# One load in eight: w1 of a decode kernel fetched as eight transfers of sixteen rows

## The chip, the cores and the metric

The kernel runs on 1 core of a Trainium2 chip. The metric is device time in microseconds (us), from one execution of the whole program; lower is better. Three runs of the kernel before took 1298.88 us each.

## What is computed

One decode step of an attention block, gated by a small MLP, for B = 2 tokens of width D = 512. H = 32 heads of 128 attend to a cache of 8192 keys and values each; everything is float32. Cut to what matters, the reference is:

```python
xn = layernorm(x)
q  = (xn @ wq).reshape(B, 1, 32, 128).transpose(0, 2, 1, 3)
p  = softmax(einsum("bhqd,bhkd->bhqk", q, k_cache) / sqrt(128))
s  = einsum("bhqk,bhkd->bhqd", p, v_cache).transpose(0, 2, 1, 3).reshape(B, 1, 4096) @ wo
y  = layernorm(xn)
h  = gelu(y @ w1 + b1)          # w1: 512 x 1376
g  = silu(h @ w2 + b2)          # w2: 1376 x 512
out = x + s * g
```

The two caches are 268 MB each, the four weights together some 22 MB. Each byte of them is used once.

## The kernel before

A list of operations is written out by hand in program order; a small planner (`Plan`) finds for each of them, from the names that it reads and writes, which semaphores of other engines or of DMAs it has to wait for, and emits each engine's operations in that order. All loads are issued by SP (`load`, line 329) into one hardware DMA queue, which the 16 DMA engines of the core work off; each load has a semaphore by the name that it is given.

The start (up to some 60 us). SP issues, without a wait, w1, x, w2, b1, b2, wq, and the two halves of the first k tile:

```python
def load(dst, src, sem, w, over=()):
    op("sp", lambda: nc.sync.dma_start(dst, src), (), w, over=over, dma=sem)
load(w1_sb, w1.rearrange("(p c) f -> p c f", p=P), "w1", ["w1"])
load(x_sb, x.rearrange("b s d -> (b s) d"), "x", ["x"])
load(w2_sb, w2.rearrange("f n -> (f n)").rearrange("(p e) -> p e", p=P), "w2", ["w2"])
```

w1 stands in SBUF as 128 partitions of 4 x 1376 numbers: partition p holds rows 4p to 4p+3 of w1, 22,016 consecutive bytes of the source. w2 has the same size (2752 KB). Both lie, with all small tiles of the MLP, inside `vb`, the buffer that later takes the v tiles; so the trace calls w1, w2, x and the biases all `vb`. w1 and w2 read there as `in_B_w_dram`, b1 and b2 as `in_B_b_dram`.

DVE and ACT make the two layer norms of x (L380 to L385), PE transposes them (L392) and ACT copies the transposes out (L393). `hidden` multiplies the second one, yT, by w1 in three column blocks of four matmuls each (L435), adds b1 (L437), turns the rows into columns (L443, L449), applies the gelu, and spreads x over partitions (L460, L478). Then PE multiplies by wq (L518), which lies in k's first buffer, repeats q over the partitions (L531, ACT's copies L533), and does the product with w2 (`outer`, L487).

The loop. The work is cut into 32 tiles, one for each token and pair of heads. A tile of k is 128 partitions of 128 keys of 128 numbers (8.4 MB); DVE multiplies it by q (L559, two halves) and sums (L566), PE, ACT and DVE make the softmax of the tile, and PE weighs the v tile (L610, 32 matmuls, each in two passes in the trace). k has two buffers, v one. SP loads v of tile n when PE has weighed v of tile n-1, and k of tile n+2 when DVE is done with tile n; `load_v` names all that lay in `vb` at the start (the list `boot`) as overwritten. The end is the load of wo in seven pieces, the matmuls with it (L690 to L711), one DVE operation (L725) and the store.

Of the kernel before, what the change touches and what calls it, by code (L numbers as in the profile page):

```python
# [21 lines left out]
class Plan:  # L22
# [18 lines left out]
    def op(self, eng, fn, r=(), w=(), over=(), it=None, loop=False, dma=None):  # L41


        o = Op()
        o.eng, o.fn, o.it, o.loop, o.dma, o.tell = eng, fn, it, loop, dma, False
        need = {}

        def after(d, war):
            if d.dma is None and dma is None and d.eng == eng and (eng == "pe" or war):
                return  # L50
            if d.dma is None:
                if need.get(d.eng) is None or need[d.eng].idx < d.idx:
                    need[d.eng] = d
            else:
                k = ("dma", d.dma)
                if need.get(k) is None or need[k].idx < d.idx:
                    need[k] = d

        for k in r:
            if k in self.writer:  # L60
                after(self.writer[k], False)
        for k in list(w) + list(over):
            if k in self.writer:
                after(self.writer[k], False)
            for d in self.readers.get(k, ()):
                after(d, True)
        clock = self.clock[eng]
        need = {k: d for k, d in need.items() if clock.get(k, 0) < d.idx}
        o.deps = [(k, d) for k, d in need.items()
                  if not any(e is not d and e.done.get(k, 0) >= d.idx for e in need.values())]  # L70
        for _, d in o.deps:
            for k, v in d.done.items():
                clock[k] = max(clock.get(k, 0), v)
        own = eng if dma is None else ("dma", dma)
        self.count[own] = o.idx = self.count.get(own, 0) + 1
        o.done = dict(clock)
        o.done[own] = o.idx
        for k in w:
            self.writer[k] = o
            self.readers[k] = []  # L80
        for k in r:
            if k not in w:
                self.readers.setdefault(k, []).append(o)
        self.ops.append(o)
# [80 lines left out]
def decode_kernel(nc, x, kc, vc, wq, wo, w1, b1, w2, b2, out):  # L165
    P = 128
    B, H, S, DH = kc.shape
    D = x.shape[2]
    F = w1.shape[1]
    ND = D // P  # L170
# [32 lines left out]
    def pe(fn, r=(), w=(), it=None, loop=False):  # L203
        op("pe", fn, r, w, it=it, loop=loop)

    def dve(fn, r=(), w=(), it=None, loop=False, over=()):
        op("dve", fn, r, w, over=over, it=it, loop=loop)

    def act(fn, r=(), w=(), it=None, loop=False):
        op("act", fn, r, w, it=it, loop=loop)  # L210
# [4 lines left out]
    def sbuf(name, shape):  # L215
        return nc.alloc_sbuf_tensor(name, shape, F32).ap()
# [8 lines left out]
    vb = sbuf("vb", [P, KP * DH])  # L225
    kbuf = [t.rearrange("p (j d) -> p j d", d=DH) for t in kb]
    vbuf = vb.rearrange("p (j d) -> p j d", d=DH)
# [45 lines left out]
    boot = []  # L273

    def take(name, p, n, base=0, at=None):

        if at is None:
            at = used[0]
            used[0] += n
            assert used[0] <= KP * DH  # L280
        boot.append(name)
        return vb[base:base + p, at:at + n]

    w1_sb = take("w1", P, ND * F).rearrange("p (c f) -> p c f", f=F)
    w2_sb = take("w2", P, WB * P)

    at = used[0]
# [16 lines left out]
    yT = take("yT", P, ND * B).rearrange("p (c b) -> p c b", b=B)  # L304
# [13 lines left out]
    def bank():  # L318
        i = turn[0] % 4
        turn[0] += 1  # L320
        return scratch[i], f"s{i}"
# [3 lines left out]
    vf = vc.rearrange("b h s d -> (b h s d)").rearrange("(n p j d) -> n p j d", p=P, j=KP, d=DH)  # L325
    M = KP // 2

    def load(dst, src, sem, w, over=()):
        op("sp", lambda: nc.sync.dma_start(dst, src), (), w, over=over, dma=sem)  # L329
# [12 lines left out]
    CUT = D - P  # L342


    load(w1_sb, w1.rearrange("(p c) f -> p c f", p=P), "w1", ["w1"])
    load(x_sb, x.rearrange("b s d -> (b s) d"), "x", ["x"])
    load(w2_sb, w2.rearrange("f n -> (f n)").rearrange("(p e) -> p e", p=P), "w2", ["w2"])
    for t, src, k in ((b1_sb, b1, "b1"), (b2_sb, b2, "b2")):
# [79 lines left out]
    def hidden():  # L428

        chunks = range(0, F, 512)  # L430
        for f in chunks:
            w = min(512, F - f)
            ph, k = bank()
            for c in range(ND):
                pe(lambda f=f, w=w, ph=ph, c=c: matmul(ph[:B, :w], yT[:, c, :], w1_sb[:, c, f:f + w],  # L435
                                                       start=(c == 0), stop=False), ["yT", "w1"], [k])
            pe(lambda f=f, w=w, ph=ph: matmul(ph[:B, :w], ones[R:R + 1, :B], b1_sb[:, f:f + w],  # L437
                                              start=False, stop=True), ["ones", "b1"], [k])
            act(lambda f=f, w=w, ph=ph: nc.scalar.copy(h_nat[:, 1 + f:1 + f + w], ph[:B, :w]),  # L439
                [k, "h_nat"], [("h_nat", f)])  # L440

        for m in range(QT):
            dve(lambda m=m: nc.vector.tensor_copy(  # L443
                h_row[:, :, m::QT],
                h_nat[:, WM * m:WM * m + WB * R].rearrange("b (k e) -> b e k", e=WB)[:, :WR, :]),
                ["h_nat"] + [("h_nat", f) for f in chunks], [("h_row", m)])
        ph, k = bank()
        for r in range(WR):
            pe(lambda r=r: transpose(ph[:, r * B:(r + 1) * B], h_row[:, r, :], ident[2 * R:2 * R + B, 2 * R:2 * R + B]),  # L449
               ["ident"] + [("h_row", m) for m in range(QT)], [k])  # L450

        act(lambda: nc.scalar.copy(h, ph[:, :WR * B].rearrange("p (r b) -> p r b", b=B)), [k], ["h"])
        dve(lambda: nc.vector.tensor_mul(u, h, h), ["h"], ["u"])
        dve(lambda: nc.vector.tensor_scalar(u, u, GELU_A, 1.0, op0=ALU.mult, op1=ALU.add), ["u"], ["u"])
        dve(lambda: nc.vector.tensor_mul(u, u, h), ["u", "h"], ["u"])
        act(lambda: nc.scalar.activation(u, u, AF.Tanh, scale=GELU_C), ["u"], ["u"])
        dve(lambda: nc.vector.scalar_tensor_tensor(u, u, 1.0, h, op0=ALU.add, op1=ALU.mult), ["u", "h"], ["u"])
        dve(lambda: nc.vector.tensor_scalar_mul(u, u, 0.5), ["u"], ["u"])
        px, kx = bank()
        pe(lambda: matmul(px, pick, x_sb, start=True, stop=True), ["pick", "x"], [kx])  # L460
        act(lambda: nc.scalar.copy(xa, px), [kx], ["xa"])

        for c in range(QT):
            for lo, hi, r, m in ((0, c + 1, 1, QT - 1 - c), (c + 1, QT, 0, 0)):
                if lo == hi:
                    continue
                parts.append(("hs", c, lo))

                def part(c=c, lo=lo, hi=hi, r=r, m=m):
                    shape = [P, WM, hi - lo, B]  # L470
                    return nc.vector.tensor_tensor(
                        out=hs[:, :, c, lo:hi, :], in0=u[:, r:r + WM, :].unsqueeze(2).to_broadcast(shape),
                        in1=cls[:, m:m + hi - lo].unsqueeze(1).unsqueeze(3).to_broadcast(shape), op=ALU.mult)
                dve(part, ["u"] + [("cls", m) for m in range(QT)], [parts[-1]])
        dve(lambda: nc.vector.tensor_tensor(
            out=xa.rearrange("p (q n) -> p q n", n=CW), in0=xa.rearrange("p (q n) -> p q n", n=CW),
            in1=slot.unsqueeze(2).to_broadcast([P, CH, CW]), op=ALU.mult), ["xa", "slot"], ["xa"])
        dve(lambda: nc.vector.tensor_reduce(out=x4, in_=xa.rearrange("p (q n) -> p n q", n=CW), axis=AX.X, op=ALU.add),  # L478
            ["xa"], ["x4"])
# [20 lines left out]
    def gates():  # L500
        dve(lambda: nc.vector.scalar_tensor_tensor(th, th, 1.0, z, op0=ALU.add, op1=ALU.mult), ["th", "z"], ["th"])
        for j in range(QT):
            dve(lambda j=j: nc.vector.tensor_scalar_mul(  # L503
                gate[R * j:R * (j + 1), :, 1], th[R * j:R * (j + 1), j * CW:(j + 1) * CW], 0.5), ["th"], [("gate", j)])

    hidden()


# [3 lines left out]
    for i in range(NQ):  # L512
        for c in range(ND):
            wv = wq_sb[:, c, :].rearrange("p (h s d) -> p h s d", s=U, d=DH)
            a = (NQ - 1 - i) * B
            for j in range(QT):
# [4 lines left out]
                    start=(i + c == 0), stop=(i == NQ - 1 and c == ND - 1)),  # L521
                   ["xnT"] + [("kb", 0, s) for s in range(2)], ["po"])
    act(lambda: nc.scalar.copy(q_nat, PO), ["po"], ["o4"])
    for k in range(N // NB):
# [3 lines left out]
        p, kp = bank()  # L528
        for s in range(U):
            a = R * (U * g + s) + B * i + b  # L530
            pe(lambda p=p, s=s, a=a: matmul(p[HP * s:HP * (s + 1), :], ident[:, a:a + 1].to_broadcast([P, HP]), q_nat,  # L531
                                            start=True, stop=True), ["ident", "o4"], [kp])
# [6 lines left out]
    load_k(1)  # L539

    def load_v(n):
        load(vbuf, vf[n], "v", ["vb"], over=boot)

    def cols(t, a, n):

# [138 lines left out]
    def piece(c, n=0):  # L684
        return ("wo", max(i for i, a in enumerate(WO_PIECES[:-1]) if a <= c) + int(c == OC - 1 and n >= CUT))


    for c in range(WIDE):
        j = c % QT
        pe(lambda c=c, j=j: matmul(wide[R * j:R * j + RM, :], on[:, :, c], wo_sb[:, c, :],  # L690
                                   start=(c < QT), stop=(c + QT >= WIDE)), ["on", piece(c)], ["wide"])
# [9 lines left out]
    for c in range(WIDE, OC - LAST):  # L701
        for j in range(QT):
            pe(lambda c=c, j=j: matmul(acc[R * j:R * j + RM, :], on[:, :, c], wo_sb[:, c, j * P:(j + 1) * P],  # L703
                                       start=False, stop=(c == OC - LAST - 1)), ["on", piece(c)], ["acc"])
# [54 lines left out]
```

## Time and profile before

| | |
|---|---|
| runs | 1298.88, 1298.88, 1298.88 us |
| profiled execution | 1298.97 us, of which the span from the first to the last instruction is 1297.70 us |
| bytes moved | 559.33 MB in the one load queue |
| busiest engines | DVE 1138.0 us, PE 411.7 us |
| granted TensorE clock, mean | 0.626 |

How to read it: a row of the timeline has start, length, engine, line, operation, tiles (out<-in) and, in brackets, the idle time ahead of it and what ended it. A row of the windows has the window and its length, then each engine's busy time and number of instructions (PE, its weight loads, DVE, ACT, POOL), the granted clock, the mean busy share of the 16 DMA engines, and GB/s. Packets count in the window in which they start, so that short windows can show a share over 1.

### The profile page before, as it was taken

Reading aid. Unit: us, or ns where it says so; the run is one execution under the profiler, and the core shown is the slowest. Engines: PE = TensorE matmul, PEld = TensorE weight load, DVE = VectorE, ACT = ScalarE, POOL = GpSimd, SP = SyncE. Lnnn points to the kernel's source line nnn. Section 1 sums busy time; section 2 is a strip of 40 time slices with the busy share of each in tenths; the row PEclk is TensorE's granted clock in tenths of the full one; section 3 lists DMA queues with packets and bytes.
Section 4 is the critical chain, followed back from the end, with each engine's and each line's share of the span. In section 5 each row is a group of like instructions: output and inputs, shape, how many; then the busy total and the mean of one; then the engine's idle time right before and its main releaser. Section 6 shows DMA issues by size and latency. Waiting matters only on the chain.

```text
span 1297.7 us, 6944 instructions
## 1 busy us (share of the span) xinstructions
PE 411.7 (32%) x2796; PEld 123.9 (10%) x2796; DVE 1138.0 (88%) x294; ACT 78.0 (6%) x250; POOL 1.4 (0%) x8
## 2 busy tenths in 40 slices
PE   5602333312333312333311333321333321333327
PEld 1100011000101000101100101000001100001103
DVE  3699999888889988889988889988888988888991
ACT  1200000000000000000000000000000000000000
POOL 0000000000000000000000000000000000000000
PEclk9856666556666556666555666655666655666659
DMA  9999999999999999999999999999999999999998
GB/s 400 449 425 440 428 428 442 426 442 426 434 438 424 446 424 440 430 426 444 426 438 430 428 442 426 442 426 432 440 424 446 424 440 430 424 446 426 427 430 373
DMA packets 11231, 559.42 MB, mean 431 GB/s; under 512 B 1364, under 2 KB 1620, under 8 KB 1880
## 3 DMA queue, kind: packets, MB, share of 16 engines
q1 hardware_dynamic: 11224, 559.33, 99.7%
q8 instruction: 4, 0.07, 0.0%
q14 instruction: 3, 0.02, 0.0%
HBM read 559.30 MB, written 0.03 MB: 431 GB/s over the span
## 4 chain that ended last, share of the span: by engine, by line
DMA 72%; PE 23%; DVE 3%; issue 1%; ACT 0%; SPq 0%; another core or an unknown queue 0%; DVEq 0%; ACTq 0%
DMA vb<-in_A_v_cache_dram 67%; PE po L610 22%; DMA kb<-in_A_wq_dram 3%; DMA vb<-in_A_wo_dram 2%; DVE kb L559 1%; DVE sc L566 1%; PE po L518 1%; SPq L329 0%; PE acc L703 0%; PE s L531 0%; PE wide L711 0%; ACT PZ L587 0%; DVE gate L503 0%; PE s L582 0%; ACT Q L533 0%
## 5 line engine op out<-in xcount | busy, mean ns | idle before, releaser
L559 DVE TENSOR_TENSOR kb<-kb,Q 128x8192 f32<-128x8192 f32 x64 | 555.6, 8682 | 107.9 <-DMA kb<-in_A_k_cache_dram 96.7
L566 DVE TENSOR_REDUCE sc<-kb 128x64 f32<-128x8192 f32 x64 | 552.3, 8666 | 0.0
L610 PE MATMUL po<-vb,PZ 128*8 128x512 f32 x1984 | 288.8, 748 | 293.7 <-DMA vb<-in_A_v_cache_dram 292.0
L582 PE MATMUL s<-nm,srow 1*128 1x2 f32 x64 | 18.4, 355 | 364.1 <-DVE nm L576 364.1
L610 PEld LDWEIGHTS po<-vb,PZ 128*8 128x8 f32 x1984 | 57.5, 104 | 499.0 <-issue 497.2
L573 PE MATMUL s<-ident,mx 128*1 128x128 f32 x32 | 11.8, 369 | 180.2 <-DVE mx L570 180.2
L582 PEld LDWEIGHTS s<-nm,srow 1*128 1x128 f32 x64 | 15.7, 302 | 373.3 <-DVE nm L576 373.3
L617 ACT COPY o<-po 128x512 f32<-128x512 f32 x32 | 18.8, 586 | 541.7 <-PE po L610 541.7
L583 ACT COPY bias<-s 128x2 f32<-128x2 f32 x32 | 5.1, 160 | 609.3 <-PE s L582 609.3
L619 PE MATMUL s<-mod,o 128*128 128x2 f32 x256 | 33.6, 253 | 22.1 <-ACT o L617 22.1
L619 PEld LDWEIGHTS s<-mod,o 128*128 128x128 f32 x256 | 31.1, 191 | 51.3 <-ACT o L617 51.3
L587 ACT ACTIVATE PZ<-sc,bias 64x128 f32<-64x128 f32 x64 | 25.5, 399 | 1.8
L573 PEld LDWEIGHTS s<-ident,mx 128*1 128x1 f32 x32 | 2.5, 79 | 183.0 <-DVE mx L570 183.0
L625 DVE TENSOR_TENSOR Z<-blk,s 128x8 f32 (+1 forms) x32 | 5.2, 163 | 12.4 <-PE s L619 12.4
L443 DVE COPY vb<-vb 2x384 f32<-2x384 f32 x4 | 1.8, 500 | 14.7 <-ACT vb L439 14.7
L587 ACT ACTIVATION_READ_ACCUMULATOR PZ<-sc,bias 64x1 f32 x64 | 11.8, 185 | 0.0
L435 PE MATMUL s<-vb 128*2 128x512 f32 (+1 forms) x24 | 11.3, 620 | 0.3 <-ACT vb L393 0.3
L570 DVE TENSOR_REDUCE mx<-sc 128x1 f32<-128x128 f32 x32 | 9.1, 286 | 1.1
L591 ACT ACTIVATE ZR<-half,rs 128x8 f32 (+1 forms) x32 | 9.6, 301 | 4.1
L518 PE MATMUL po<-kb,vb 128*4 128x512 f32 x64 | 8.4, 684 | 2.6 <-DMA kb<-in_A_wq_dram 2.6
L610 PE MATMUL po<-kb,PZ 128*8 128x512 f32 x64 | 8.8, 709 | 1.4 <-ACT PZ L587 1.4
L576 DVE TENSOR_REDUCE nm<-s 1x2 f32<-1x128 f32 x32 | 8.7, 272 | 0.3 <-PE s L573 0.3
(101 smaller groups left out, 80.7 us busy)
## 6 DMA issues: line engine op xcount, KB each, us to landing
kb<-in_A_k_cache_dram SPq DMA_DIRECT2D x4, 4096.0 KB, 43.3
kb<-in_A_v_cache_dram SPq DMA_DIRECT2D x2, 4096.0 KB, 40.4
vb<-in_B_w_dram SPq DMA_DIRECT2D x2, 2752.0 KB, 12.3
vb<-in_A_wo_dram SPq DMA_DIRECT2D x1, 4096.0 KB, 19.8
vb<-in_A_wo_dram SPq DMA_DIRECT2D x1, 2048.0 KB, 24.3
vb<-in_A_wo_dram SPq DMA_DIRECT2D x1, 1280.0 KB, 26.9
vb<-in_A_wo_dram SPq DMA_DIRECT2D x2, 256.0 KB, 27.0
vb<-in_A_v_cache_dram SPq DMA_DIRECT2D x31, 29.2
```

The costliest lines, as they stand in the source:

```text
L435: pe(lambda f=f, w=w, ph=ph, c=c: matmul(ph[:B, :w], yT[:, c, :], w1_sb[:, c, f:f + w], start=(c == 0), stop=False), ["yT", "w1"], [k])
L518: pe(lambda i=i, c=c, wv=wv, a=a, j=j, hd=hd: matmul(PO[R * j:R * j + NQ * B, :].rearrange("m (h d) -> m h d", d=DH), xnT[:, c, a:a + NQ * ...
L559: vector(n, n, lambda n: nc.vector.tensor_tensor(out=k, in0=k, in1=cols(Q, n * DH, DH).unsqueeze(1).to_broadcast([P, M, DH]), op=ALU.mult) ...
L566: vector(n, n, lambda n: nc.vector.tensor_reduce(out=SC[:, s * M:(s + 1) * M], in_=k, axis=AX.X, op=ALU.add), [("kb", i, s)], [("sc", s)])
L570: vector(n, n, lambda n: nc.vector.tensor_reduce(out=MX, in_=SC, axis=AX.X, op=ALU.max), [("sc", 0), ("sc", 1)], ["mx"])
L573: pe(lambda i: transpose(PM[:1, :P], MX, ident), ["mx", "ident"], ["s1"], it=n, loop=n > 0)
L582: pe(lambda i: matmul(PN[:, :U], srow, NM, start=True, stop=True), ["srow", "nm"], ["s2"], **one)
L587: act(lambda i, r=r, s=s: nc.scalar.activation(PZ[r, :, s, :], sc[r], AF.Exp, bias=BIAS[r, s:s + 1], scale=SCALE, accum_out=RS[r]), ["bias ...
L591: act(lambda i: nc.scalar.activation(cols(ZR, i * UP - UP, UP), half, AF.Copy, scale=RS), ["half"] + [("rs", s) for s in range(U)], [("ZR" ...
L610: pe(lambda i, t=t, j=j, v=v: matmul(PO[R * j:R * j + U * JW, :], PZ[:, t].rearrange("p s j -> p (s j)"), v[:, t * JW:(t + 1) * JW, :].rea ...
L617: act(lambda i: nc.scalar.copy(O4, PO), ["po"], ["o4"], **one)
L619: pe(lambda i, k=k: matmul(PT[:, :U], O4[:, k * DH:(k + 1) * DH], mod[:, k:U * JW:JW], start=(k == 0), stop=(k == JW - 1)), ["o4", "mod"], ...
```

## The change

w1 is fetched by eight DMAs in place of one. Transfer r takes partitions r, r+8, ..., r+120, sixteen rows of 22,016 bytes, and has a semaphore and a name of its own, so that the rows, the bytes and their places in SBUF are the same. What reads w1, and what overwrites it, names all eight.

```diff
-    w1_sb = take("w1", P, ND * F).rearrange("p (c f) -> p c f", f=F)
+    w1_flat = take("w1", P, ND * F)
+    w1_sb = w1_flat.rearrange("p (c f) -> p c f", f=F)
...
-    load(w1_sb, w1.rearrange("(p c) f -> p c f", p=P), "w1", ["w1"])
+    RE = P // 16
+    w1_r = w1.rearrange("(p c) f -> p (c f)", p=P)
+    for r in range(RE):
+        load(w1_flat[r::RE], w1_r[r::RE], f"w1{r}", [("w1", r)])
...
             for c in range(ND):
                 pe(lambda f=f, w=w, ph=ph, c=c: matmul(ph[:B, :w], yT[:, c, :], w1_sb[:, c, f:f + w],
-                                                       start=(c == 0), stop=False), ["yT", "w1"], [k])
+                                                       start=(c == 0), stop=False),
+                   ["yT"] + [("w1", r) for r in range(RE)], [k])
...
-        load(vbuf, vf[n], "v", ["vb"], over=boot)
+        load(vbuf, vf[n], "v", ["vb"], over=boot + [("w1", r) for r in range(RE)])
```

On SP, the queue's first rows before are these (the first is w1, the third w2):

```order
L329 DMA vb<-in_B_w_dram 128x5504 [waits barrier_Pool_Activation_PE_DVE_SP_release]
L329 DMA vb<-in_A_x_dram 2x512
L329 DMA vb<-in_B_w_dram 128x5504
L329 DMA vb<-in_B_b_dram 1x1376
L329 DMA vb<-in_B_b_dram 1x512
L329 DMA kb<-in_A_wq_dram 128x16384
L329 DMA kb<-in_A_k_cache_dram 128x8192 x2
L329 DMA kb<-in_A_k_cache_dram 128x16384 [waits pe]
L329 DMA vb<-in_A_v_cache_dram 128x16384 [waits dve]
```

and now:

```order
L330 DMA vb<-in_B_w_dram 16x5504 [waits barrier_Pool_Activation_PE_DVE_SP_release]
L330 DMA vb<-in_B_w_dram 16x5504 x7
L330 DMA vb<-in_A_x_dram 2x512
L330 DMA vb<-in_B_w_dram 128x5504
L330 DMA vb<-in_B_b_dram 1x1376
L330 DMA vb<-in_B_b_dram 1x512
L330 DMA kb<-in_A_wq_dram 128x16384
L330 DMA kb<-in_A_k_cache_dram 128x8192 x2
L330 DMA kb<-in_A_k_cache_dram 128x16384 [waits pe]
L330 DMA vb<-in_A_v_cache_dram 128x16384 [waits dve]
```

Seven issues more stand ahead of x and all that follows it; the first load of v, and every other one, waits for the same as before.

On PE, from the transposes to the gelu's, before:

```order
L392 MATMUL s<-ident,vb 128x2 [waits dve]
L392 MATMUL s<-ident,vb 128x2 x3
L435 MATMUL s<-vb 2x512 [waits act,dma_w1]
L435 MATMUL s<-vb 2x512 x3
L437 MATMUL s<-vb,ones 2x512 [waits dma_b1]
L435 MATMUL s<-vb 2x512 x4
```

and now:

```order
L396 MATMUL s<-ident,vb 128x2 [waits dve]
L396 MATMUL s<-ident,vb 128x2 x3
L439 MATMUL s<-vb 2x512 [waits dma_w15,dma_w14,dma_w16,dma_w13,dma_w17,dma_w12,act,dma_w11,dma_w10]
L439 MATMUL s<-vb 2x512 x3
L442 MATMUL s<-vb,ones 2x512 [waits dma_b1]
L439 MATMUL s<-vb 2x512 x4
```

The order of the matmuls is the same; the first one that reads w1 waits for eight transfers (dma_w10 to dma_w17) in place of one. No other engine's order or waits differ.

## The prediction

> **What bounds the kernel now.** I read the page first, for the engine that is full; then the chain of waits at both ends of the span, for what the end hangs on; then windows over the DMA columns, for the pace of the stream in each stage.
>
> ```profile
> span 1297.7 us, 6944 instructions
> PE 411.7 (32%) x2796; PEld 123.9 (10%) x2796; DVE 1138.0 (88%) x294; ACT 78.0 (6%) x250; POOL 1.4 (0%) x8
> DMA  9999999999999999999999999999999999999998
> GB/s 400 449 425 440 428 428 442 426 442 426 434 438 424 446 424 440 430 426 444 426 438 430 428 442 426 442 426 432 440 424 446 424 440 430 424 446 426 427 430 373
> q1 hardware_dynamic: 11224, 559.33, 99.7%
> DMA 72%; PE 23%; DVE 3%; issue 1%; ACT 0%; SPq 0%; another core or an unknown queue 0%; DVEq 0%; ACTq 0%
> ```
>
> The one DMA queue that SP feeds fills its 16 engines for 99.7% of the span; DVE, the fullest engine, has 88%. All slices lie within a few per cent of 434 GB/s, but for the first (400) and the last (373). The chain says the same at both ends:
>
> ```profile
> 2.56 33.50 DMA kb<-in_A_wq_dram
> 36.11 8.44 PE po L518 x64
> ...
> 1227.59 28.83 DMA vb<-in_A_v_cache_dram
> 1256.54 9.21 PE po L610 x64
> ...
> 1266.61 26.91 DMA vb<-in_A_wo_dram
> 1293.56 1.28 PE acc L703 x40
> 1295.86 0.29 DVE res L725
> ```
>
> These are start, length and what held the chain. At the start it hangs on wq (33.5 us), at the end on v and on wo, after which only some 2.5 us of matmuls, one DVE operation and the store are left. The 23% of PE in the chain are not a second bound, since the queue has work while they run:
>
> ```profile
> 2.96 41.93 SPq L329 DMA_DIRECT2D kb<-in_A_k_cache_dram  x3
> 66.35 0.33 SPq L329 DMA_DIRECT2D vb<-in_A_v_cache_dram  x1
> 83.66 0.33 SPq L329 DMA_DIRECT2D kb<-in_A_k_cache_dram  x1
> 104.93 0.33 SPq L329 DMA_DIRECT2D vb<-in_A_v_cache_dram  x1
> ```
>
> ```profile
> kb<-in_A_k_cache_dram SPq DMA_DIRECT2D x1, 31.0
> ```
>
> The first four rows are SP's issues in the timeline, the last, from the list of DMA issues, the time to landing of the k tile issued at 83.66: it lands at 114.7, and the v load behind it was issued at 104.9, 9.7 us ahead. So the stream never runs dry, and whatever is lost in it at the start is added to the end, in full: there is no later idle time of DMA in which to catch up. The question is thus only what the change does to the 16 engines during the first 10 us.
>
> ```profile
> 0.00:1.77 1.77, 0.00 (x0) 0.00 (x0) 0.78 (x12) 1.04 (x1) 1.01 (x7) 1.00 0.00 0
> 1.75:3.30 1.55, 0.00 (x0) 0.00 (x0) 1.20 (x3) 0.47 (x2) 0.42 (x2) 1.00 0.97 227
> 4.10:9.02 4.92, 0.00 (x0) 0.00 (x0) 1.67 (x12) 0.00 (x0) 0.00 (x0) 1.00 1.00 430
> 9.02:15.55 6.53, 1.74 (x9) 1.22 (x10) 4.07 (x15) 0.80 (x4) 0.00 (x0) 1.00 1.01 432
> 16.40:33.00 16.60, 14.28 (x43) 2.77 (x41) 2.31 (x7) 2.47 (x5) 0.00 (x0) 0.97 1.00 434
> 100.00:1200.00 1100.00, 323.00 (x2153) 97.01 (x2145) 1002.41 (x202) 57.40 (x197) 0.00 (x0) 0.61 1.00 434
> ```
>
> The last two columns are the DMA engines' busy share and GB/s. Nothing moves before 1.77. From 1.75 to 3.30 the engines hold packets but move 227 GB/s: the ramp costs 1.55 x (1 - 227/430) = 0.73 us. Then w1 (to 9.0), w2 (to 15.5), wq and the k and v tiles run at 430 to 434 GB/s, 26.9 to 27.1 for each of 16 engines. A w1 row of 22,016 bytes takes one engine 22,016 / 26.9 = 0.82 us, and each engine has 8 of them: 6.55 us.
>
> **The change part by part.**
>
> Seven more DMAs on SP. The issues there:
>
> ```profile
> 0.74 0.39 SPq L329 DMA_DIRECT2D vb<-in_B_w_dram  x1
> 1.18 0.32 SPq L329 DMA_DIRECT2D vb<-in_A_x_dram  x1
> 1.56 0.34 SPq L329 DMA_DIRECT2D vb<-in_B_w_dram  x1
> 1.94 0.58 SPq L329 DMA_DIRECT2D vb<-in_B_b_dram  x2
> 2.56 0.35 SPq L329 DMA_DIRECT2D kb<-in_A_wq_dram  x1
> ```
>
> One issue takes 0.3 to 0.4 us, with 2 rows or with 128, and they follow each other every 0.4 us. Seven more put x, w2, b1, b2, wq and the two halves of k(0) some 2.8 us later: x is issued at about 4.0, w2 at 4.4, k(0) by 6.8. Each piece gives an engine 0.82 us of work for 0.4 us of issue, so the pieces queue up faster than they drain, and the engines reach x and w2 only at 9.0: 4.6 us of cover. If rows drained in less than 0.4 us the issue would be the bound; they cannot at 27 GB/s. Cost 0.
>
> Seven more completions on each DMA engine. No row shows eight small loads in a row; the nearest are w1 and w2, the same bytes behind one another with x between them (size, time from issue to landing):
>
> ```profile
> vb<-in_B_w_dram SPq DMA_DIRECT2D x1, 2752.0 KB, 9.4
> ...
> vb<-in_B_w_dram SPq DMA_DIRECT2D x1, 2752.0 KB, 15.1
> ```
>
> w1 lands at 0.74 + 9.4 = 10.1, w2 at 1.56 + 15.1 = 16.7. Those are 6.5 us for 2.818 MB, which at 430 GB/s take 6.55: a border between transfers costs less than the rounding, 0.1 us. Seven: 0 to 0.7 us, and I take 0.
>
> Eight semaphores instead of one on PE, ahead of the first matmul of the hidden layer, and the later arrival of x in the first case below:
>
> ```profile
> 9.71 0.68 DVE L380 BATCH_NORM_STATS2 vb<-vb 2x6 f32<-2x512 f32 x1 [3.50 <-DMA vb<-in_A_x_dram]
> 15.08 5.21 PE L435 MATMUL s<-vb 128*2 128x512 f32 x8 [0.35 <-ACT vb L393]
> 32.42 1.05 PE L460 MATMUL s<-vb,pick 2*128 2x512 f32 x1
> 35.85 1.02 DVE L478 TENSOR_REDUCE x<-vb 128x32 f32<-128x512 f32 x1
> 36.11 8.38 PE L518 MATMUL po<-kb,vb 128*4 128x512 f32 x64 [2.63 <-DMA kb<-in_A_wq_dram]
> 47.44 8.69 DVE L559 TENSOR_TENSOR kb<-kb,Q 128x8192 f32<-128x8192 f32 x1 [10.57 <-ACT Q L533]
> ```
>
> The first hidden matmul waits last for ACT's copy of yT (15.08), 5 us after w1. Seven more waits stand in PE's queue ahead of all the hidden matmuls; at 0.05 us each (an estimate, from the 0.02 to 0.12 us of "issue" in the chain) they are 0.35 us, and PE then idles 2.63 us for wq. DVE's end of that chain (36.87) has 10.57 us of idle time before L559. If w1 comes late by d, x, queued behind it, and wq come late by the same d, so both covers keep their size. Cost 0. The v load gains eight names to wait for, all read by PE work that it waits for already, so no new wait is issued: 0.
>
> The rows that are in flight together. Before, one transfer has all 128 rows and the hardware gives each engine eight; after, each transfer has 16 partitions, 8 apart. The trace shows no load of such a shape, so it is bounded. From below: if each engine gets the rows that it had, or if it makes no difference where 16 rows land, a row stays at 0.82 us; and the ramp of 0.73 us could shrink, as a first transfer with an eighth of the rows may start all engines sooner: -0.7 to 0. From above: the pace is the same 27 GB/s per engine for w1, w2, wq, k and v, rows of 22 or of 64 KB, so it is set not by the tensor read but by the engine or its way into SBUF. No part of SBUF is seen to take more than one engine's 27 GB/s, because every large load spreads over all 128 partitions at once. If the partitions of one new transfer fall two to a way, two engines share 27 GB/s in every piece, since every engine works at the same piece: a row takes 1.64 us, and w1 8 x 0.82 = 6.5 us longer. The ramp may hide it in the first row: 7 x 0.82 = 5.7. Larger shares, four to a way, would give 24 x 0.82 = 19.6.
>
> I take the pairwise sharing, 6.1 us (the middle of 5.7 and 6.5): for the pace to hold, a way into SBUF would have to take 54 GB/s, twice the most that any row shows, while engines whose pace is alike to 1% whatever they read look matched to what takes their data. That partitions 8 apart share a way is the weak link; no row of the trace shows which engine writes which partition.
>
> [...]
>
> The sum: 0 + 0 + 0 + 6.1 = +6.1 us on the profiled execution's 1298.97 (span 1297.70 and 1.27 around it): 1305.1. The median of the runs is 0.09 lower: 1305.0.
>
> **The rivals.**
>
> Not slower: the 16 rows keep their pace. For it: the 128-row load may already hand each engine rows in the same order, so the same partitions are in flight together; the waits added are covered. Against: what was said on 54 GB/s. The time is 1298.88 - 0.7 (no ramp) to + 0.7 (seven borders), 1298.2 to 1299.6, most likely 1298.8. It decides in the first 10 us: if w1's last piece lands near 10, it is this one.
>
> Each transfer pays its own start. From issue to landing w1 takes 9.4 us for 6.55 us of data, 2.9 us around it. Were these paid by each piece in turn, it would be 7 x 2.9 = +20 us: 1319. Against it stands w2, which lands 6.5 us behind w1 with the start paid in the shadow. [...]
>
> Less or more than pairs: engines that started apart (the ramp ends at different times) drift to different pieces and share only partly, +1 to +5 us, 1300 to 1304; or four share, 1318.
>
> **How the numbers follow.** About 0.2% (2.6 us) is what a measurement of this kernel can tell from no change. Pairwise sharing 0.60 (1304.3 to 1306.0, "slower"); pace kept 0.30 ("same", all within 0.7 us); partly shared 0.06 (two thirds of it beyond 2.6 us, "slower"); four to a way or each piece's own start 0.03; gains beyond the ramp, unseen in any row, 0.01. That gives slower 0.67, same 0.32, faster 0.01. The likeliest gives 1305.0, its own range 1304.3 to 1306.0; the range that holds 8 in 10 has to reach to the kept pace: 1298.5 to 1306.0.
>
> **What would show it.** In the windows from 2 to 16 us the GB/s should fall to some 215 to 230 while the DMA share stays at 1.00, and return to 430 behind w1; w1's last piece should land near 16, L380 start near 15.8, wq's wait end near 42 and the later chain be the same, 6 us later. GB/s of 430 from 4 us on and L380 at 9.7 would refute the sharing. A DMA share well under 1 between pieces would mean that issue or completions starve the engines, where I costed nothing. Any difference that arises after 45 us would be outside all of this.

## The result, and the profile after

The changed kernel takes 1305.8 us (1305.72 to 1306.0, 6 runs) where the kernel before took 1298.9 us in the same job: a ratio of 1.0053, 95% interval 1.0042 to 1.0064. It is 6.9 us slower. The forecast was 1305.0 us, slower.

The page of the changed kernel, against the lines shown of before:

```profile
span 1304.5 us, 6954 instructions
DMA  9999999999999999999999999999999999999998
GB/s 334 417 443 424 444 424 442 426 440 428 432 436 426 442 424 442 424 444 424 444 424 444 424 444 424 444 424 442 424 442 424 444 424 442 426 438 430 423 432 373
q1 hardware_dynamic: 11336, 559.33, 99.7%
DMA 72%; PE 23%; DVE 3%; issue 1%; SPq 1%; ACT 0%; DVEq 0%; ACTq 0%
```

The bytes are the same, the queue has 112 packets more (all of them under 512 bytes, 1476 against 1364; 16 for each of the seven transfers more), and it is still busy for 99.7% of the span. What differs is the first of the 40 slices: 334 GB/s in place of 400. 66 GB/s less over 32.6 us are 2.2 MB, some 5 us of the stream; neighbouring slices differ by up to 20 GB/s anyway, so this gives the place and the rough size. A busy share of 99.7% in both tells nothing of it: the share adds up the times of the packets, and a packet that takes twice as long counts as busy for twice as long (from 4.1 to 9.0 us the share is 0.97 at 206 GB/s, and before it was 1.00 at 430).

The windows show where it is:

```profile
0.00:2.10 2.10, 0.00 (x0) 0.00 (x0) 0.84 (x12) 1.36 (x2) 1.34 (x8) 1.00 0.00 0
4.10:9.02 4.92, 0.00 (x0) 0.00 (x0) 1.66 (x12) 0.00 (x0) 0.00 (x0) 1.00 0.97 206
9.02:15.55 6.53, 0.00 (x0) 0.00 (x0) 0.00 (x0) 0.00 (x0) 0.00 (x0) 1.00 1.00 216
15.60:22.40 6.80, 1.67 (x9) 1.22 (x10) 4.07 (x15) 0.80 (x4) 0.00 (x0) 1.00 1.00 424
100.00:1200.00 1100.00, 324.06 (x2174) 97.83 (x2174) 1006.01 (x199) 58.86 (x203) 0.00 (x0) 0.61 1.00 433
```

From 4.1 to 15.6 us, while w1 comes in, the engines move 206 to 216 GB/s at a share of 0.97 to 1.00; before, it was 430 at 1.00. With w2, again in one transfer of 128 rows, the pace is back at 424. The other loss is in the first row: nothing has started by 2.10. In the kernel before, the same window had this:

```profile
0.00:2.10 2.10, 0.00 (x0) 0.00 (x0) 0.84 (x12) 1.36 (x2) 1.34 (x8) 1.00 0.50 105
```

SP's issues, the landing times (in the list of DMA issues, of the first and of the last piece of w1, and of w2), and those who wait:

```profile
0.74 5.04 SPq L330 DMA_DIRECT2D vb<-in_B_w_dram  x8
5.82 0.48 SPq L330 DMA_DIRECT2D vb<-in_A_x_dram  x1
6.34 0.36 SPq L330 DMA_DIRECT2D vb<-in_B_w_dram  x1
7.37 0.35 SPq L330 DMA_DIRECT2D kb<-in_A_wq_dram  x1
```

```profile
vb<-in_B_w_dram SPq DMA_DIRECT2D x1, 344.0 KB, 4.4
...
vb<-in_B_w_dram SPq DMA_DIRECT2D x1, 344.0 KB, 11.4
...
vb<-in_B_w_dram SPq DMA_DIRECT2D x1, 2752.0 KB, 16.8
```

```profile
16.63 0.68 DVE L384 BATCH_NORM_STATS2 vb<-vb 2x6 f32<-2x512 f32 x1 [10.43 <-DMA vb<-in_A_x_dram]
22.00 5.83 PE L439 MATMUL s<-vb 128*2 128x512 f32 x8 [0.35 <-ACT vb L397]
42.64 9.19 PE L523 MATMUL po<-kb,vb 128*4 128x512 f32 x64 [2.24 <-DMA kb<-in_A_wq_dram]
54.79 8.69 DVE L564 TENSOR_TENSOR kb<-kb,Q 128x8192 f32<-128x8192 f32 x1 [10.36 <-ACT Q L538]
...
1302.69 0.29 DVE res L730
```

The first piece lands at 0.74 + 4.4 = 5.1. The eighth is issued at 5.19 (by the chain of waits) and lands 11.4 later, at 16.6. Seven pieces in 11.5 us are 1.64 us for a row, twice 0.82. w1 is complete 6.4 us later than before (10.2), w2 6.4 us later (6.34 + 16.8 = 23.1 against 16.7), PE gets wq 6.5 us later (42.64 against 36.11), and the last DVE operation comes 6.8 us later (1302.69 against 1295.86; the last line is of the chain).

### The profile page after: what moved, and what is told of

Its sections match the earlier page's. It is cut to its first block, busy times and chain, and to the rows that moved or that the text cites. A ratio compares the mean times of both kernels' runs of the same rounds, so it can differ in the third digit from the quotient of the medians.

```text
span 1304.5 us, 6954 instructions
## 1 busy us (share of the span) xinstructions
PE 409.3 (31%) x2796; PEld 123.7 (9%) x2796; DVE 1137.9 (87%) x294; ACT 78.0 (6%) x250; POOL 1.4 (0%) x8
## 2 busy tenths in 40 slices
DMA packets 11343, 559.42 MB, mean 429 GB/s; under 512 B 1476, under 2 KB 1732, under 8 KB 1992
## 3 DMA queue, kind: packets, MB, share of 16 engines
q1 hardware_dynamic: 11336, 559.33, 99.7%
## 4 chain that ended last, share of the span: by engine, by line
DMA 72%; PE 23%; DVE 3%; issue 1%; SPq 1%; ACT 0%; DVEq 0%; ACTq 0%
DMA vb<-in_A_v_cache_dram 67%; PE po L615 22%; DMA kb<-in_A_wq_dram 3%; DMA vb<-in_A_wo_dram 2%; DVE kb L564 1%; DVE sc L571 1%; PE po L523 1%; SPq L330 1%; PE acc L708 0%; PE s L536 0%; PE wide L716 0%; ACT PZ L592 0%; DVE gate L508 0%; PE s L587 0%; ACT Q L538 0%
## 5 line engine op out<-in xcount | busy, mean ns | idle before, releaser
L564 DVE TENSOR_TENSOR kb<-kb,Q 128x8192 f32<-128x8192 f32 x64 | 555.5, 8681 | 107.2 <-DMA kb<-in_A_k_cache_dram 96.2
L615 PE MATMUL po<-vb,PZ 128*8 128x512 f32 x1984 | 284.9, 739 | 293.7 <-DMA vb<-in_A_v_cache_dram 292.0
L439 PE MATMUL s<-vb 128*2 128x512 f32 (+1 forms) x24 | 12.0, 649 | 0.3 <-ACT vb L397 0.3
## 6 DMA issues: line engine op xcount, KB each, us to landing
vb<-in_B_w_dram SPq DMA_DIRECT2D x1, 2752.0 KB, 16.8
```

The source lines that it names most:

```text
L564: vector(n, n, lambda n: nc.vector.tensor_tensor(out=k, in0=k, in1=cols(Q, n * DH, DH).unsqueeze(1).to_broadcast([P, M, DH]), op=ALU.mult) ...
L615: pe(lambda i, t=t, j=j, v=v: matmul(PO[R * j:R * j + U * JW, :], PZ[:, t].rearrange("p s j -> p (s j)"), v[:, t * JW:(t + 1) * JW, :].rea ...
```

## The experiments

All runs were timed in three rounds beside the kernel before, which took 1298.88 us in the first job and 1298.84 in the second. Three theories stood at the start: (1) the rows in flight go to places in SBUF that share a way, the prediction's word for a path by which partitions take data from the engines, which no trace names; (2) each transfer has a price; (3) the stride in the source is slow to read.

**Eight transfers that each cover all partitions.**

```diff
-        load(w1_flat[r::RE], w1_r[r::RE], f"w1{r}", [("w1", r)])
+        cs = slice(r * ND * F // RE, (r + 1) * ND * F // RE)
+        load(w1_flat[:, cs], w1_r[:, cs], f"w1{r}", [("w1", r)])
```

> Eight transfers again, but each of all 128 partitions and one eighth of the columns (2752 bytes a row). Theory 1 (engines share a way into SBUF when the 16 partitions in flight fall two to a way): nothing is shared, so the stream keeps 430 GB/s and the time is that of the kernel before, 1298.9, plus at most 0.6 us for 56 more packets and borders on each engine. Theory 2 (each transfer pays a price of its own, 7 times some 0.9 us): 1305 to 1306. Theory 3 (rows of the source 176 KB apart, read at one time, are slow to read): no such rows here, 1299.

It took 1300.24 us, ratio 1.0010 (1.0001 to 1.0020): +1.4 us, more than theory 1 gave (at most 0.6) and far from theory 2's. The last piece lands at 4.0 + 7.1 = 11.1, 1.0 us later than w1 before, and the pace did not quite hold: 366 GB/s where it had been 430. The edit changes two things, the number of transfers and the rows (2752 bytes each, eight times as many), and no run tells them apart; so the number of transfers explains 1.4 us at most.

```profile
vb<-in_B_w_dram SPq DMA_DIRECT2D x1, 344.0 KB, 7.1
...
4.10:9.02 4.92, 0.00 (x0) 0.00 (x0) 1.66 (x12) 0.00 (x0) 0.00 (x0) 1.00 1.01 366
```

**Sixteen consecutive partitions to a transfer.**

```diff
-        load(w1_flat[r::RE], w1_r[r::RE], f"w1{r}", [("w1", r)])
+        rs = slice(16 * r, 16 * r + 16)
+        load(w1_flat[rs], w1_r[rs], f"w1{r}", [("w1", r)])
```

> Eight transfers of 16 consecutive partitions, 16r to 16r+15, with their 16 consecutive source rows. [...] With a layout of one way for 8 neighbours it would be eight engines to a way, 1298.9 + 45.8 = 1345. Theory 2 (price per transfer): as with the change, 1305.8. Theory 3 (source stride): consecutive rows, 1299 to 1300.

It took 1315.23 us, ratio 1.0125 (1.0108 to 1.0142), +16.4 us: the slowest, as neither of the other theories has it, though 3.2 us less than the 19.6 that the prediction gave for four to a way. First and last piece:

```profile
0.74 3.62 SPq L330 DMA_DIRECT2D vb<-in_B_w_dram  x8
...
vb<-in_B_w_dram SPq DMA_DIRECT2D x1, 344.0 KB, 5.2
...
vb<-in_B_w_dram SPq DMA_DIRECT2D x1, 344.0 KB, 22.7
```

The first lands at 5.9, the eighth, issued at 3.9, at 26.6: 2.96 us a row, and not the 4 x 0.82 = 3.28 of four engines at one engine's pace. Sixteen rows of 22,016 bytes in 2.96 us are 119 GB/s. That is 3.6 times slower than the 430 of before. The 1345 us of eight engines to a way are out.

**The same partitions as in the change, another source.**

```diff
-        load(w1_flat[r::RE], w1_r[r::RE], f"w1{r}", [("w1", r)])
+        load(w1_flat[r::RE], w1_r[16 * r:16 * r + 16], f"w1{r}", [("w1", r)])
```

> As the change, partitions 8 apart in each transfer, but each transfer reads 16 consecutive rows of the source; rows of w1 so come to other partitions than those that the MLP's arithmetic means, with the same amount of work. Theory 1 (place in SBUF): 1305.8 as with the change. Theory 2: 1305.8. Theory 3 (source stride): 1299.

It took 1305.67 us, ratio 1.0051 (1.0035 to 1.0068): the change's time. Its windows read as the change's do, so the source's stride has no part in it:

```profile
4.10:9.02 4.92, 0.00 (x0) 0.00 (x0) 1.66 (x12) 0.00 (x0) 0.00 (x0) 1.00 0.96 201
9.02:15.55 6.53, 0.00 (x0) 0.00 (x0) 0.00 (x0) 0.00 (x0) 0.00 (x0) 1.00 0.96 206
```

**w2 split in place of w1.**

```diff
-    load(w2_sb, w2.rearrange("f n -> (f n)").rearrange("(p e) -> p e", p=P), "w2", ["w2"])
+    w2_r = w2.rearrange("f n -> (f n)").rearrange("(p e) -> p e", p=P)
+    for r in range(RE):
+        load(w2_sb[r::RE], w2_r[r::RE], f"w2{r}", [("w2", r)])
```

> w1 in one transfer as before, and w2, of the same size, in eight transfers of partitions 8 apart. Theory 1: the loss is that of the shared rows alone, 8 x 0.81 = 6.4 to 6.5 us, without the 0.4 us by which the first packet came later in the change: 1305.3 to 1305.5. If the loss came from starting the stream with a small strided transfer, w2 in its shadow would lose less than 1 us: 1299 to 1300.

It took 1306.29 us, ratio 1.0057 (1.0040 to 1.0073): +7.4 us, so the loss is not one of starting the stream. It is 1 us more than expected. The landings of w1 and of w2's last piece (issued at 6.0), and the window in which w1 comes in:

```profile
vb<-in_B_w_dram SPq DMA_DIRECT2D x1, 2752.0 KB, 10.3
...
vb<-in_B_w_dram SPq DMA_DIRECT2D x1, 344.0 KB, 18.5
...
4.10:9.02 4.92, 0.00 (x0) 0.00 (x0) 1.66 (x12) 0.00 (x0) 0.00 (x0) 1.00 1.03 434
```

w1, untouched, lands at 11.0 and not at 10.2, but that is not where the loss is: it came in at 434 GB/s, and by the times of the packets all engines but one are done with it by 9.5 (before, all by 9.8). The last one is late; by then the others already write w2's rows, and whether that is the reason is not shown. The loss lies in w2, where every sixteen rows pay, the first sixteen too, and in the first row of wq behind it, which takes 3.09 us on average in place of 2.42 (row times are below).

Place in SBUF was left. The second set asked which partitions cost time when one transfer holds them, and whether the size of the transfer matters.

**Four and two partitions apart.**

```diff
+        hv, q = divmod(r, 4)
+        rs = slice(64 * hv + q, 64 * hv + 64, 4)
+        load(w1_flat[rs], w1_r[rs], f"w1{r}", [("w1", r)])
```

> Eight transfers of 16 partitions, 4 apart, within one half of the partitions: 0, 4, ..., 60, then 1, 5, ..., 61 and so on, later the same from 64 up. [...]

1305.62 us, ratio 1.0052 (1.0035 to 1.0069), with 201 to 213 GB/s from 4.1 to 15.6 us: sixteen partitions 4 apart in one half cost what sixteen 8 apart over the whole range do.

```diff
+        hv, q = divmod(r, 2)
+        rs = slice(32 * hv + q, 32 * hv + 32, 2)
+        load(w1_flat[rs], w1_r[rs], f"w1{r}", [("w1", r)])
```

> Eight transfers of 16 partitions, 2 apart, within 32 neighbours: 0, 2, ..., 30, then 1, 3, ..., 31, then the same from 32, 64 and 96 up. [...]

1305.84 us, ratio 1.0054 (1.0037 to 1.0070), with 197 to 210 GB/s: the same price again.

**Two halves.**

```diff
-    RE = P // 16
+    RE = 2
...
+        rs = slice(64 * r, 64 * r + 64)
+        load(w1_flat[rs], w1_r[rs], f"w1{r}", [("w1", r)])
```

> Two transfers, partitions 0 to 63 and 64 to 127, 1.4 MB each. [...] If the loss had to do with small or strided transfers, these are neither: 1299 to 1299.5.

1306.12 us, ratio 1.0056 (1.0039 to 1.0072). Two transfers of 1.4 MB, each of consecutive rows, lose as much as eight small ones: the first lands at 0.74 + 9.6 = 10.3, the second, issued at 1.36, 15.6 us later at 17.0.

```profile
vb<-in_B_w_dram SPq DMA_DIRECT2D x1, 1376.0 KB, 9.6
...
vb<-in_B_w_dram SPq DMA_DIRECT2D x1, 1376.0 KB, 15.6
...
4.10:9.02 4.92, 0.00 (x0) 0.00 (x0) 1.66 (x12) 0.00 (x0) 0.00 (x0) 1.00 1.02 215
```

**Thirty-two partitions, four apart, over all 128.**

```diff
-    RE = P // 16
+    RE = P // 32
```

> [...]

1299.59 us, ratio 1.0006 (0.9997 to 1.0016): +0.75 us, at the edge of what can be told from none (the fastest of its ten runs took 1299.34, the slowest of before 1299.08). One number in the changed kernel, and the pace is back:

```profile
4.10:9.02 4.92, 0.00 (x0) 0.00 (x0) 1.66 (x12) 0.00 (x0) 0.00 (x0) 1.00 1.00 425
9.02:15.55 6.53, 1.50 (x9) 1.22 (x10) 4.07 (x15) 0.80 (x4) 0.00 (x0) 1.00 1.01 432
...
36.18 9.11 PE L523 MATMUL po<-kb,vb 128*4 128x512 f32 x64 [2.46 <-DMA kb<-in_A_wq_dram]
```

wq arrives at 36.18, against 36.11 before. Partitions 4 apart were slow in half of the range (201 to 213 GB/s) and keep the pace when each transfer takes 32 of them over the whole of it. The records name no engine's partition, so which of the 32 rows are written at one time is not shown.

**What each set of partitions cost.** The pace is that of the window from 4.10 to 9.02 us, in which w1 comes in, and the cost is against the kernel before:

| partitions of one transfer | transfers | GB/s | cost, us |
|---|---|---|---|
| all 128 (the kernel before) | 1 | 430 | 0 |
| 32, 4 apart, over the whole range | 4 | 425 | +0.75 |
| all 128, an eighth of the columns | 8 | 366 | +1.4 |
| 64 consecutive | 2 | 215 | +7.3 |
| 16, 8 apart, over the whole range (the change) | 8 | 206 | +6.9 |
| 16, 4 apart, in one half | 8 | 201 | +6.8 |
| 16, 2 apart, within 32 neighbours | 8 | 197 | +7.0 |
| 16 consecutive | 8 | 98, then 125 to 15.55 us | +16.4 |

So the cost goes with the partitions that a transfer holds. It does not go with the number of transfers (eight cost 1.4 or 16.4 us) or with their size (1376 KB cost 7.3 us, 688 KB 0.75). That engines share a way, two of them at half the pace and four at little over a quarter, is the author's estimate from the pace. How many ways there are, and which partitions belong to one, these runs do not show.

No version was faster than the kernel before, and none of these points to one.

## Why the prediction was right

**The stream never runs dry, so a loss at the start comes back in full.** It held in four runs: w1 complete 1.0, 6.4 and 16.5 us later (columns, the change, consecutive partitions) gave +1.4, +6.9 and +16.4 us, and with w2 split wq's 7.5 us (43.6 against 36.1) gave +7.4. Differences of up to half a microsecond remain, the change's own last 0.3 us between wq and the end among them; no run settles these.

**The shared rows: 6.1 us.** The loss came in the stage and at the pace that were forecast, and was 0.3 us larger. A row took 1.64 us between landings, as forecast for two to a way, and the pace in the windows was 206 to 216 GB/s (215 to 230 forecast). The traces also hold the start and length of every packet, and each row of w1, w2 and wq is one packet. In order of start, sixteen at a time (as many as there are engines), their mean lengths in us are:

| | w1, 1st row | w1, 2nd to 8th | w2, 1st row | w2, 2nd to 8th | wq, 1st row |
|---|---|---|---|---|---|
| before | 1.50 | 0.82 to 0.84 | 0.82 | 0.82 | 2.42 |
| the change | 1.49 | 1.51 to 1.70 | 1.28 | 0.82 to 0.83 | 2.42 |
| w2 split | 1.54 | 0.82 to 0.84 | 1.41 | 1.54 to 1.71 | 3.09 |
| 16 consecutive | 2.03 | 2.96 to 2.99 | 1.82 | 0.82 | 2.42 |

The ramp hid the first row, as the prediction's lower bound of 5.7 has it. The other seven of the change took 5.9 us more than before, and w2's first row 0.5 more, which the prediction left out: w2's first rows start from 14.8 us on, while the last row of w1 ends at 16.0. That is 6.4 us, and the signs came with it: x's norm starts at 16.63 (15.8 forecast), the wait for wq ends at 42.64 (near 42 forecast). The rows kept their 1.70 to the last piece, so the engines did not drift apart into partial sharing. The weak link, that partitions 8 apart fall two to a way, was taken at 0.60 with no row of before to show it; what the runs bore out is that place decides: 16 consecutive partitions lose most (+16.4 us), 16 in steps of 2, 4 and 8 lose the same (+6.8 to +7.0), 32 over the whole range lose almost nothing (+0.75), and the source does not matter (1305.67 us against 1305.8). That the place is a way with two engines on it remains the author's estimate, from the 1.64 us of a row against 0.82.

**The ramp: -0.7 to 0.** This had the wrong sign. The first row took as long as before, and the first transfer started later: no packet by 2.10, where the kernel before has its engines at work from 1.77. The fewer rows are not the reason, since 16 consecutive partitions start as early as before:

```profile
0.00:1.77 1.77, 0.00 (x0) 0.00 (x0) 0.78 (x12) 1.04 (x1) 1.01 (x7) 1.00 0.08 12
```

The first sixteen rows start 0.2 us later on average than before (2.26 against 2.08). The 0.8 us that the sum lacked (1305.0 against 1305.8) are so 0.3 of the shared rows, 0.2 of the start, and 0.3 behind wq that stay open.

**Seven issues: cost 0, at 0.4 us each.** The size was off: eight took 5.04 us, 0.63 each, so x was issued at 5.82 and not at 4.0. The cover held, as the engines reached x only behind w1 (its norm starts at 16.63, w1 lands at 16.6). At w1's old pace of 0.82 us a row it would have been thin: 0.2 us for each piece.

**Seven completions: 0 to 0.7, taken as 0.** Not separated in the change. Four transfers of 32 partitions, with three completions more, brought wq 0.1 us later, start included, which points to far less than 0.7 for seven.

**PE's eight waits: 0.** Right: L439 comes 5.4 us behind the first norm as L435 did (22.00 - 16.63, before 15.08 - 9.71), PE still idles 2.24 us for wq and DVE 10.36 us ahead of L564 (2.63 and 10.57 before).

The rivals: the kept pace is out by the windows. A start paid by each transfer is out by the eight transfers over all partitions, at +1.4 us. Size did not decide here: 0.34 MB pieces behind one another cost 1.4 us when they cover all partitions, and 1.4 MB pieces cost 7.3 us when they do not. That is the reverse of what size alone would tell.

## What to carry to other kernels

Where DMA is the bound, ask of every load not only how large it is but which partitions are in flight at one time: here a load of one half of the partitions (215 GB/s), or of every eighth one (206 to 216), ran at half the pace of 430, and one of 16 neighbours at little over a quarter (119), all with the 16 engines shown as busy (1.00 to 1.07 from 9.02 to 15.55 us). Look at GB/s beside the busy share, by windows of the stage; a share of 1.00 with half the GB/s was this here. If a load has to be cut, cut it by columns (+1.4 us here for eight pieces), or by rows 4 apart over all 128 partitions (+0.75 us for four).

## What the runs showed of the hardware that was not expected

- An issue's time on SP did not follow the number of rows in these runs. The first issue took 0.55 to 0.63 us for 16 or 32 partitions with a step and for 64 consecutive ones, and 0.39 for 16 consecutive ones and for all 128. The first packet came later with it: at 2.09 to 2.14 us with the longer issues, at 1.75 to 1.77 with the shorter. Why is not shown.
- Sixteen rows to 16 consecutive partitions took 2.98 us, less than four times the 0.82 of a row at full pace (3.28), while rows to partitions 8 apart took 1.70, more than twice (1.64). Why is not shown.
- In all six runs at half pace, the fifth of the eight rows was quicker, 1.50 to 1.57 us in place of some 1.70. Why stays open.
